# Ten orders of a step for the first 23 steps of a fused attention and two-MoE kernel, output banks freed of each other's copies, the tenth mask on TensorE, and the embeddings' norms moved to the first two steps

## The chip, the cores and the metric

The kernel runs on one core of a Trainium2 chip as one program. The time is that of the device in microseconds (us), the median of three runs. The engines are named as the profile names them: PE (TensorE's matmuls), PEld (its weight loads), DVE (VectorE), ACT (ScalarE), POOL (GpSimd) and SP (SyncE, which issues most DMAs).

## The reference

Three stages follow each other, all in float32.

```python
# 1: attention, 4 batches x 8 heads, 576 positions, 64 wide, only the 32 largest scores of a row
scores = matmul(q, k.transpose(0, 1, 3, 2)) / sqrt(64)
kth    = partition(scores, -32)[..., -32:-31]          # the 32nd largest of each row
attn   = softmax(where(scores >= kth, scores, -1e9))
x      = matmul(attn, v)  ->  2304 tokens x 512
# 2: first MoE: a dense layer 512 -> 2048 -> 512
h = x @ w_in
x = (h * clip(h + 3, 0, 6) / 6) @ w_out
# 3: second MoE: 8 experts, each token goes to one
logits = normalised(x) @ normalised(expert_emb).T / tau
e      = argmax(logits);  gate = softmax(logits)[e]
out    = gate * (relu(x @ w1[e]) @ w2[e])
```

## The kernel before

**Stages.** Attention and the first MoE run together in a loop of 76 steps; behind it comes the tail with the routing's last part and the experts. There are 72 units of attention, one a step: a unit is 256 rows (two tiles of 128) of a batch and head against its 576 keys. Step i works on several units at once:

- unit i: the scores by TensorE into PSUM (`scores`, L456 to L469), a copy of half of the columns to SBUF by ACT (`take`, L476 on ACT), and DVE's `pairs` (L485 to L489), which orders columns by two and so prepares the search of the 32nd largest;
- unit i-1: the search itself on DVE (`select`, L504 MAX8 and L507), and `bounds` on POOL (L512, L514), which makes the threshold;
- unit i-2: `relu` on ACT (L518, the op `bend`), `mask` on POOL (L533), or, for units below `VEILED` = 9, `veil` on TensorE instead (L526, L527), which adds the same term with matmuls into a PSUM bank;
- unit i-3: the exponentials on ACT (L541), the sums' inverse, and `scale` (none for units below 8, on ACT at L557 for units 8 to 15, on POOL at L559 from 16 on);
- unit i-4: transposes on TensorE (`turned`, L570), their copies by ACT (`keep`, L575), the product with the values (`values`, L591/L596) and the normalising into the first MoE's input (`finish`, L603 to L649).

**The first MoE.** Its products are made of three float32 matmuls each (high by high, high by low, low by high part). Groups of 256 tokens go through it, one after the other, each in eight parts q; from step 12 a step does one q: `s1` (L681, the hidden units), `gate` (ACT, L689), `swish` (DVE, L693), `large` (ACT, L697), `small` (POOL, L700), and a step later `s2` (L716), the output. `s2` keeps two output banks, `bank_y[:, 0]` and `bank_y[:, 1]`, one for each 128 of the 256 tokens, and adds 6 matmuls to each a q, 48 in all. At q = 7 the bank is finished and ACT copies it: `out_y(o)` is called right behind the last matmuls of bank o, with the copy at L734 (for the last group L728). There are nine groups.

**The weights.** In steps 0 to 32 the weights of the first MoE are loaded and split into high and low parts by DVE (`w_one`, L262 or L264; `w_two`, L274), ACT (`w_round`, L282, and `w_hi`, L296) and POOL (`w_add`, L288; `w_low`, L300), and the low parts go back to memory (L304), from which they are fetched as they are needed (L321).

**The order.** Each engine does its instructions in the order in which the program lists them. The scheduler changes none: the loop stands under a manual schedule, and `step` calls the ops one after another as a string of words says. The words are the ops above with their part's number (`take1` is the second half's copy, `s20` and `s21` are `s2` on bank 0 and 1, `load0` a weight's DMA, `load_k` that of a key, `lows` the casts of a key and query at L438 to L445 and L382/L383). There are strings for step 0, 1 to 2, 3 to 11, 12 to 15, 16 to 20, and then one for odd and one for even steps.

```python
names = (ZERO if i == 0 else FEW if i < 3 else FIRST if i < MOES else MID if i < 16
         else NEXT if i < WORDS else ODD if i % 2 else THEN).split()
for name in names:
    ops[name]()
```

**Waits between tiles.** A semaphore wait is put in where an instruction uses a tile that another engine wrote or read. `bank_y` is one tile with both banks.

**The embeddings.** The eight expert embeddings are normalised early: `embed` in five parts behind steps 4, 18, 19, 20 and 21 (their DMAs, the squares on ACT, a product with ones on TensorE, a square root at L200 on ACT, three small operations of DVE). The square root needs another table of functions on ACT than the exponentials.

Of the kernel before, what the change touches and what calls it, by code (L numbers as in the profile page):

```python
# [40 lines left out]
SIGNED = (4, 6, 8, 10, 12, 14, 16, 18)  # L41
VEILED = 9
PLAIN = 1
# [3 lines left out]
BEGUN = (0, 1, 2, 3, 5, 7, 9, 11, 13, 15, 17, 19, 21, 22, 24, 25, 27, 28, 30, 31, 32)  # L47
ZERO = ("turn0 s10 values s11 round0 lows xh5 pick0 load_k one1 mask0 gate xh s20 one0 aside xl swish need_v pick1 ship prep "
       "expo0 hi1 two0 score0 bend0 expo1 large round1 s21 turn1 small take0 keep0 veil1 score1 load0 turn2 load_q guard low1 "
       "pairs load1 add0 inverse xl5 xe5 two1 hi0 scale low0 keep1 mask1 bounds store0 veil0 store1 pick2 bend1 pick3 keep2 "  # L50
       "take1 xe add1 ")
FEW = ("pick0 one1 one0 lows bend1 s10 bend0 values turn0 veil1 s11 s20 round0 keep0 two0 load_k add0 turn1 xh aside mask0 "
       "score0 pick1 xh5 keep1 expo0 xl5 hi1 pick2 ship xl expo1 s21 load0 take0 low1 gate hi0 guard need_v mask1 keep2 inverse "
       "xe5 round1 two1 turn2 swish low0 add1 prep large load1 load_q veil0 score1 store0 xe pick3 scale store1 bounds take1 "
       "small pairs ")
FIRST = ("s10 turn0 expo0 load_k s11 xh5 veil1 one1 s20 round0 turn1 keep0 round1 score0 lows one0 expo1 two0 load0 turn2 guard "
       "gate swish two1 take0 pick0 pick1 aside keep1 pick2 keep2 score1 add0 ship bend0 values xl5 hi0 xh veil0 add1 inverse "
       "take1 pick3 low0 bend1 need_v xe5 xl hi1 load1 s21 mask0 scale pairs xe store0 low1 mask1 large small store1 bounds prep "
       "load_q ")
MID = ("expo0 pick0 turn0 turn1 s10 score0 load_k one0 round0 two0 one1 pick1 two1 keep0 add0 keep1 turn2 expo1 s11 take0 s20 "  # L60
       "load0 hi0 round1 lows guard score1 ship keep2 values low0 pick2 pick3 need_v inverse bend0 load1 add1 gate bend1 scale "
       "mask0 swish large bounds store0 mask1 s21 prep aside xh hi1 pairs low1 xl load_q xe small store1 take1 ")
NEXT = ("one0 expo0 round0 turn0 lows turn1 two0 s10 one1 s11 keep0 keep1 turn2 expo1 round1 bend0 score0 keep2 two1 load0 pick0 "
       "gate add0 guard hi0 values add1 pick1 take0 pick2 mask0 s20 inverse ship hi1 swish low0 low1 score1 load1 xh bend1 large "
       "scale pick3 load_k xl small mask1 bounds prep store0 s21 take1 aside store1 need_v pairs load_q xe ")
THEN = ("lows pick0 turn0 expo0 keep0 ship expo1 pick1 bend0 s10 guard turn1 place pick2 inverse score0 mask0 turn2 s11 take0 "
# [3 lines left out]
       "take0 swish values expo1 load_k score1 guard need_v pick3 bounds take1 large aside inverse s20 s21 scale small xh pairs "  # L70
       "prep xl load_q")
HS = S // 2
QS = S // 4
# [45 lines left out]
def layers(tc: tile.TileContext, qt, kt, v, w_in, w_out, embt, tau, w1, w2, out, y_dram, yq_dram, g_dram, tbl, xq_dram, lo_dram, flag, pools, consts):  # L119
# [59 lines left out]
    emb = {}  # L179

    def embed(part):

        if part == 0:
            emb["et"] = fs.tile([128, 4, E], F32, tag="df", name="et")
            nc.sync.dma_start(out=emb["et"], in_=embt.rearrange("(p k) e -> p k e", k=4))
            emb["tb"] = fs.tile([128, 1], F32, tag="gt", name="tb")
            nc.sync.dma_start(out=emb["tb"], in_=tau.rearrange("(o t) -> o t", o=1).broadcast_to([128, 1]))
        elif part == 1:
            emb["ones"] = mp.tile([128, DM], F32, tag="wf", name="onesf", bufs=4)[:, :128]
            nc.gpsimd.memset(emb["ones"], 1.0)  # L190
            emb["sq"] = fs.tile([128, 4, E], F32, tag="tmp", name="sq")
            nc.scalar.activation(emb["sq"], emb["et"], AF.Square)
        elif part == 2:
            onesf, sq = emb["ones"], emb["sq"]
            emb["pe"] = pe = half_a()
            for k in range(4):
                nc.tensor.matmul(pe[:, :E], onesf, sq[:, k, :], start=(k == 0), stop=(k == 3))
        elif part == 3:
            emb["nr"] = fs.tile([128, E], F32, tag="nrm", name="nr")
            nc.scalar.activation(emb["nr"], emb["pe"][:, :E], AF.Sqrt)  # L200
        else:
            nr = emb["nr"]
            nc.vector.tensor_scalar(nr, nr, 1e-6, emb["tb"][:, 0:1], op0=ALU.add, op1=ALU.mult)
            nc.vector.reciprocal(nr, nr)
            nc.vector.tensor_tensor(ent, emb["et"], nr.unsqueeze(1).broadcast_to([128, 4, E]), op=ALU.mult)
# [456 lines left out]
    def push_group(X, gs):  # L662
# [39 lines left out]
        def s2(q, part=None):  # L702
# [6 lines left out]
            for o in range(len(gs)):  # L709
# [3 lines left out]
                for a in range(2):  # L713
                    f = 2 * q + a
                    for n, (x, w) in enumerate(((gh, wh[:, f, :]), (gh, wl[:, a, :]), (gl, wh[:, f, :]))):
                        nc.tensor.matmul(state["y"][o], x[:, a, c], w, start=(f == 0 and n == 0), stop=(f == 15 and n == 2))  # L716
                if q == 7:
# [6 lines left out]
        def out_y(o):  # L724
            final = gs[o] >= NG - 2
            if final:
                t = late["xg"].tile([128, DM], F32, tag="xg", name="ysl")
                nc.scalar.copy(t, state["y"][o])  # L728
                nc.sync.dma_start(out=y_dram[128 * gs[o]:128 * gs[o] + 128, :], in_=t)
                finals.append((t, gs[o]))  # L730
                return
            if o == 0:
                state["t"] = stg.tile([128, 2, DM], F32, tag="st", name="ysb")
            nc.scalar.copy(state["t"][:, o, :], state["y"][o])  # L734
            if o == 1:
# [217 lines left out]
    def step(i, last):  # L953
# [23 lines left out]
        def after(o):  # L977
            if last:
# [5 lines left out]
                   guard=lambda: at_(3, guard), inverse=lambda: at_(3, inverse), scale=lambda: at_(3, scale), bounds=lambda: at_(1, bounds),  # L984
                   pairs=lambda: at_(0, pairs), values=lambda: both(values, False), xh5=lambda: fifth(finish), xl5=lambda: fifth(finish_low), xe5=lambda: fifth(finish_early), xh=lambda: both(finish), xl=lambda: both(finish_low), xe=lambda: both(finish_early))
        for n in range(2):
            ops["veil" + str(n)] = lambda n=n: at_(2 + n, veil, n)
# [8 lines left out]
        for name, f, j in (("load", w_load, -1), ("one", w_one, 0), ("two", w_two, 0), ("round", w_round, 0), ("add", w_add, 0),  # L996
                           ("hi", w_hi, 0), ("low", w_low, 0), ("store", w_store, 0)):
            for c in range(2):
                ops[name + str(c)] = lambda f=f, j=j, c=c: pair(f, j, c)
        names = (ZERO if i == 0 else FEW if i < 3 else FIRST if i < MOES else MID if i < 16 else NEXT if i < WORDS else ODD if i % 2 else THEN).split()  # L1000
        for name in names:
            ops[name]()
        if i in (4, 18, 19, 20, 21):
            embed((4, 18, 19, 20, 21).index(i))
        if i == 0:
# [9 lines left out]
    if True:  # L1015
        last = None
        with tc.manual_schedule():
            load_k(0)
            load_q(0, nc.scalar)
            w_load(0)  # L1020
            load_k(1)
# [3 lines left out]
            nc.gpsimd.tensor_scalar(tri, ident, -1.0, None, op0=ALU.mult)  # L1025
            nc.vector.memset(half, 0.5)
            nc.gpsimd.memset(kb[:, :, 0], -SCALE)
            nc.gpsimd.memset(kb[:, :, 1], BIG)
# [471 lines left out]
```

## Time and profile before

| what | value |
| --- | --- |
| median of three runs | 1011.04 us (1010.49 to 1011.4) |
| the profiled execution's own time | 1010.06 us |
| its span, first to last instruction | 1008.3 us |
| mean granted TensorE clock | 0.990 |
| busy: PE, PEld | 947.1 us (94%), 824.4 us (82%) |
| busy: DVE, ACT, POOL | 771.6 us (77%), 709.8 us (70%), 624.5 us (62%) |

The profiled execution stands 0.98 us below the median, and 1.8 us of it lie outside the span. A step is placed by the start of `pairs` in the trace: that of unit 0 starts at 6.68 us, of unit 15 at 142.13, of unit 19 at 190.35, of unit 22 at 219.56. The loop ends at about 725 us. The span in 40 slices of 25 us shows PE under 90% busy in the first seven and in the last one, and at 90% or more in all others; the shares by stage stand in the rows below.

### The profile page before, as it was taken

Reading aid. Unit: us, or ns where it says so; the run is one execution under the profiler, and the core shown is the slowest. Engines: PE = TensorE matmul, PEld = TensorE weight load, DVE = VectorE, ACT = ScalarE, POOL = GpSimd, SP = SyncE. Lnnn points to the kernel's source line nnn. Section 1 sums busy time; section 2 is a strip of 40 time slices with the busy share of each in tenths; the row PEclk is TensorE's granted clock in tenths of the full one; section 3 lists DMA queues with packets and bytes.
Section 4 is the critical chain, followed back from the end, with each engine's and each line's share of the span. In section 5 each row is a group of like instructions: output and inputs, shape, how many; then the busy total and the mean of one; then the engine's idle time right before and its main releaser. Section 6 shows DMA issues by size and latency. Waiting matters only on the chain. (4 is left out here: it accounts for less than half of the span.)

```text
span 1008.3 us, 20945 instructions
## 1 busy us (share of the span) xinstructions
PE 947.1 (94%) x7270; PEld 824.4 (82%) x7270; DVE 771.6 (77%) x2348; ACT 709.8 (70%) x1443; POOL 624.5 (62%) x793
## 2 busy tenths in 40 slices
PE   4787788999999999999999999999999999999997
PEld 2454577889889989988988888788898988999997
DVE  7999997889989989989989889882134455666661
ACT  5899898888789778789778777775334454555551
POOL 4799888867778788678688666666232453134310
PEclk9999799999999999999999999999999999999999
DMA  7666567653456654456565466466497567667730
GB/s 252 215 190 196 188 209 247 232 185 130 160 164 190 231 183 142 151 162 212 204 182 142 138 225 202 139 225 203 154 267 245 133 225 255 227 202 238 245 153 23
DMA packets 100691, 193.24 MB, mean 192 GB/s; under 512 B 16189, under 2 KB 42448, under 8 KB 100575
## 3 DMA queue, kind: packets, MB, share of 16 engines
q1 hardware_dynamic: 95983, 181.74, 55.8%
q0 software_dynamic: 4448, 10.00, 3.2%
q8 instruction: 59, 0.97, 0.4%
q14 instruction: 57, 0.47, 0.2%
q10 hardware_dynamic: 144, 0.07, 0.0%
HBM read 163.64 MB, written 24.92 MB: 187 GB/s over the span
## 5 line engine op out<-in xcount | busy, mean ns | idle before, releaser
L533 POOL TENSOR_TENSOR s<-s,z 128x576 f32<-128x576 f32 x126 | 162.5, 1290 | 62.5 <-ACT z L518 61.7
L681 PE MATMUL bank_h<-xh,vh 128*128 128x256 f32 x576 | 172.1, 299 | 0.0
L681 PE MATMUL bank_h<-xh,lo 128*128 128x256 f32 x576 | 164.3, 285 | 0.0
L681 PE MATMUL bank_h<-xl,vh 128*128 128x256 f32 x576 | 164.0, 285 | 0.0
L504 DVE MAX8 A<-left 128x8 f32<-128x288 f32 (+1 forms) x288 | 159.9, 598 | 0.0
L716 PE MATMUL bank_y<-wh,gh 128*128 128x512 f32 x288 | 117.6, 408 | 6.7 <-ACT ysb L734 6.0
L575 ACT COPY pt<-bank_t 128x384 f32<-128x384 f32 x216 | 101.6, 480 | 25.7 <-PE bank_t L570 25.6
L700 POOL TENSOR_TENSOR gl<-u,gh 128x512 fp32r<-128x512 f32 x72 | 93.3, 1296 | 42.0 <-ACT gh L697 41.8
L518 ACT ACTIVATE z<-s,nb 128x576 bf16<-128x576 f32 x144 | 112.9, 785 | 5.0 <-POOL nb L512 4.7
L570 PE MATMUL bank_t<-both,s 128*128 128x128 f32 x648 | 103.6, 277 | 13.0 <-ACT s L557 10.2
L716 PE MATMUL bank_y<-lo,gh 128*128 128x512 f32 x288 | 113.8, 395 | 0.0
L716 PE MATMUL bank_y<-wh,gl 128*128 128x512 f32 x288 | 113.4, 394 | 0.0
L681 PEld LDWEIGHTS bank_h<-xh,vh 128*128 128x128 f32 x576 | 111.4, 193 | 0.5 <-issue 0.2
L681 PEld LDWEIGHTS bank_h<-xl,vh 128*128 128x128 f32 x576 | 111.5, 194 | 0.3
L476 ACT COPY s<-ps_sc 128x576 f32<-128x576 f32 x143 | 92.3, 646 | 27.3 <-PE ps_sc L469 11.3
L681 PEld LDWEIGHTS bank_h<-xh,lo 128*128 128x128 f32 x576 | 111.0, 193 | 0.2 <-DMA lo<-lo_dram 0.2
L570 PEld LDWEIGHTS bank_t<-both,s 128*128 128x128 f32 x648 | 77.6, 141 | 35.7 <-ACT s L557 13.6
L541 ACT ACTIVATE s<-s,nb 128x576 f32<-128x576 f32 x126 | 99.1, 787 | 0.9 <-POOL s L533 0.9
L1118 POOL DMA_INDIRECT out_dram<-ob,idt x20 | 23.7, 1186 | 121.4 <-ACT ob L1111 81.6
L559 POOL TENSOR_SCALAR s<-s,sums 128x576 f32<-128x576 f32 x112 | 82.3, 746 | 18.1 <-DVE sums L548 17.6
L689 ACT ACTIVATE u<-bank_h,half 128x512 f32<-128x512 f32 x72 | 49.9, 693 | 61.8 <-PE bank_h L681 57.0
L941 DVE TENSOR_TENSOR l<-a,h 128x1024 fp32r<-128x1024 f32 x64 | 77.3, 1241 | 17.2 <-ACT h L939 17.2
(287 smaller groups left out, 2687.2 us busy)
## 6 DMA issues: line engine op xcount, KB each, us to landing
lo<-lo_dram SPq DMA_DIRECT2D x144, 512.0 KB, 4.8
a<-in_moe_w_dram SPq DMA_DIRECT2D x64, 512.0 KB, 6.7
vt<-in_v_dram SPq DMA_DIRECT2D x28, 320.0 KB, 5.3
w<-in_moe_w_in_dram SPq DMA_DIRECT2D x16, 512.0 KB, 4.6
lo_dram<-wf SPq DMA_DIRECT2D x32, 256.0 KB, 2.2
w<-in_moe_w_out_dram SPq DMA_DIRECT2D x16, 512.0 KB, 4.8
qraw<-in_q_dram SPq DMA_DIRECT2D x48, 128.0 KB, 4.1
krs<-in_k_dram SPq DMA_DIRECT2D x16, 288.0 KB, 4.1
```

Of the source, the lines that this page charges most:

```text
L476: nc.scalar.copy(sbuf[i % NS][:, :, HS * g:HS * g + HS], ps_[i][:, :, :HS])
L504: nc.vector.max(A[:, n, 8 * r:8 * r + 8], src[:, n, :w])
L518: nc.scalar.activation(zb_[n], tile_of(i, n), AF.Relu, bias=sel[i][1][:, n, 1:2], scale=-BIG)
L533: nc.gpsimd.tensor_tensor(s, s, zb_[n], op=ALU.subtract)
L541: nc.scalar.activation(s, x, AF.Exp, bias=sel[i][1][:, n, 0:1], scale=SCALE, accum_out=sums[i][:, n:n + 1])
L559: nc.gpsimd.tensor_scalar(x, x, rv[:, n:n + 1], 1.0, op0=ALU.mult, op1=ALU.mult)
L570: nc.tensor.transpose(pp[:, 128 * k:128 * k + 128], e[:, 128 * (3 * c + k):128 * (3 * c + k) + 128], ident)
L575: nc.scalar.copy(pts[i][:, 3 * c:3 * c + 3, :].rearrange("p k n -> p (k n)"), tb_.pop((i, c))[:, :384])
L681: nc.tensor.matmul(ph[:, a, :], w, x[:, k, :], start=(k == 0 and n == 0), stop=(k == 3 and n == 2))
L700: nc.gpsimd.tensor_tensor(state[q][1], state.pop((q, "u")).rearrange("p (a n) -> p a n", a=2), state[q][0].bitcast(F32), op=ALU.subtract)
L716: nc.tensor.matmul(state["y"][o], x[:, a, c], w, start=(f == 0 and n == 0), stop=(f == 15 and n == 2))
L941: nc.vector.tensor_tensor(lo, x, hi.bitcast(F32), op=ALU.subtract)
```

## The change

Four things change.

1. **Orders.** The five strings for steps 0 to 20 give way to ten, for steps 0; 1 to 2; 3 to 9; 10 to 11; 12 to 13; 14 to 15; 16 to 17; 18 to 20; 21; 22. From step 23 on the two strings are as before. The ops are the same; what each string changes is the order in which every engine finds them.
2. **Banks.** The matmuls of `s2` on one bank are declared independent of the copies that read the other bank.
3. **Tenth mask.** `VEILED` goes from 9 to 10: unit 9's mask, two instructions of POOL, becomes 8 matmuls of TensorE.
4. **Embeddings.** The DMAs of the embeddings are issued from ACT's queue ahead of the loop, the ones lie in a tile that is used otherwise only later, the squares are made ahead of the loop, and the product, the square root and a first use of the exponential (which brings its table back) are an op `root` in step 1. The last part stays behind step 21.

```diff
-VEILED = 9
+VEILED = 10
...
-ZERO = ("turn0 s10 values s11 round0 lows xh5 pick0 load_k one1 mask0 gate xh s20 one0 aside xl swish need_v pick1 ship prep "
...
+ORDERS = ((1, "turn0 lows one1 load0 pick0 ship keep0 score0 turn1 bend1 load_k hi1 xh5 s20 pick1 aside mask0 one0 values xh "
...
         if part == 0:
             emb["et"] = fs.tile([128, 4, E], F32, tag="df", name="et")
-            nc.sync.dma_start(out=emb["et"], in_=embt.rearrange("(p k) e -> p k e", k=4))
+            nc.scalar.dma_start(out=emb["et"], in_=embt.rearrange("(p k) e -> p k e", k=4))
...
         elif part == 1:
-            emb["ones"] = mp.tile([128, DM], F32, tag="wf", name="onesf", bufs=4)[:, :128]
+            emb["ones"] = norm_[:, 0, :128]
...
             nc.scalar.activation(emb["nr"], emb["pe"][:, :E], AF.Sqrt)
+            nc.scalar.activation(emb["sq"][:, 0, 0:1], half, AF.Exp)
...
-                        nc.tensor.matmul(state["y"][o], x[:, a, c], w, start=(f == 0 and n == 0), stop=(f == 15 and n == 2))
+                        w_ = nc.tensor.matmul(state["y"][o], x[:, a, c], w, start=(f == 0 and n == 0), stop=(f == 15 and n == 2))
+                        tc.declare_no_dep(w_.ins, group=f"bank {1 - o} {exact}", reason="the other bank is read")
...
-                nc.scalar.copy(t, state["y"][o])
+                w_ = nc.scalar.copy(t, state["y"][o])
+                tc.add_to_no_dep_group(f"bank {o} {exact}", w_.ins)
...
-            nc.scalar.copy(state["t"][:, o, :], state["y"][o])
+            w_ = nc.scalar.copy(state["t"][:, o, :], state["y"][o])
+            tc.add_to_no_dep_group(f"bank {o} {exact}", w_.ins)
...
+        ops["root"] = lambda: (embed(2), embed(3)) if i == 1 else None
...
-        names = (ZERO if i == 0 else FEW if i < 3 else FIRST if i < MOES else MID if i < 16 else NEXT if i < WORDS else ODD if i % 2 else THEN).split()
+        names = next((o for n, o in ORDERS if i < n), ODD if i % 2 else THEN).split()
         for name in names:
             ops[name]()
-        if i in (4, 18, 19, 20, 21):
-            embed((4, 18, 19, 20, 21).index(i))
+        if i == 21:
+            embed(4)
...
             load_q(0, nc.scalar)
+            embed(0)
             w_load(0)
...
             nc.vector.memset(half, 0.5)
+            embed(1)
```

On TensorE, at the eighth part of the second group (`s2`, L716; three rows to each of the 16 hidden blocks, `gh` and `gl` are the parts of the activations), the program of before has this. The last three rows of bank 0, then bank 1's six, then the transposes:

```order
L716 MATMUL bank_y<-wh,gh 128x512
L716 MATMUL bank_y<-lo_3375,gh 128x512
L716 MATMUL bank_y<-wh,gl 128x512
L716 MATMUL bank_y<-wh,gh 128x512 [waits Activation_49]
L716 MATMUL bank_y<-lo_3375,gh 128x512
L716 MATMUL bank_y<-wh,gl 128x512
L716 MATMUL bank_y<-wh,gh 128x512
L716 MATMUL bank_y<-lo_3375,gh 128x512
L716 MATMUL bank_y<-wh,gl 128x512
L570 MATMUL bank_t_119<-both,s_143 128x128 [waits Pool_49]
```

The same place now (L716 is now L737, L570 is L591):

```order
L737 MATMUL bank_y<-wh,gh 128x512
L737 MATMUL bank_y<-lo_3381,gh 128x512
L737 MATMUL bank_y<-wh,gl 128x512
L737 MATMUL bank_y<-wh,gh 128x512
L737 MATMUL bank_y<-lo_3381,gh 128x512
L737 MATMUL bank_y<-wh,gl 128x512
L737 MATMUL bank_y<-wh,gh 128x512
L737 MATMUL bank_y<-lo_3381,gh 128x512
L737 MATMUL bank_y<-wh,gl 128x512
L591 MATMUL bank_t_119<-both,s_143 128x128 [waits Pool_49]
```

The rows stay where they are; the wait of bank 1's first matmul for ACT is gone.

On ACT, in step 16 of before: from the last copies of transposes, by both halves of unit 16's scores (L476), to the first row behind them (`z` is made by `relu`, `u` and `gh` belong to the first MoE, `s_142` at L557 is the scale of unit 13, `qh` and `kst` are casts of the next query and key):

```order
L575 COPY pt<-bank_t_119 128x384
L689 ACTIVATE u<-bank_h,half 128x512
L296 CAST wh<-wf 128x512
L476 COPY s_141<-ps_sc 128x2x288
L518 ACTIVATE z_148<-s_143,nb 128x576
L697 CAST gh<-u 128x512
L557 ACTIVATE s_142<-s_142,sums 128x576 x2
L438 CAST qh<-qraw 128x256
L382 CAST kst<-kraw 128x576
L383 CAST kst<-kraw 128x576
L476 COPY s_141<-ps_sc 128x2x288
L541 ACTIVATE s_143,sums<-s_143,nb 128x576
```

Step 16 now (L689 is L710, L296 is L317, L476 is L497, L518 is L539, L697 is L718, L557 is L578, L438 is L459, L382 is L403):

```order
L539 ACTIVATE z_148<-s_143,nb 128x576
L539 ACTIVATE z_147<-s_143,nb 128x576
L596 COPY pt<-bank_t_118 128x384
L497 COPY s_141<-ps_sc 128x2x288
L596 COPY pt<-bank_t_119 128x384
L317 CAST wh<-wf 128x512
L710 ACTIVATE u<-bank_h,half 128x512
L459 CAST qh<-qraw 128x256
L403 CAST kst<-kraw 128x576
L404 CAST kst<-kraw 128x576
L497 COPY s_141<-ps_sc 128x2x288
L718 CAST gh<-u 128x512
```

Between the two copies of scores stood `z`, `gh` and the two scales beside the casts; now `z` stands ahead of both and `gh` and the scales (the two rows behind the last one shown) behind both. In the same step `load_k`, the key's DMA on SP, moves from behind the two weight loads to ahead of them.

On POOL, steps 11 and 12 of before (`s` at L533 is the mask of unit 9, `norm` and `xl` are the first MoE's input, `wf` weights, `nb` the thresholds):

```order
L632 TENSOR_TENSOR norm<-norm 128x128
L533 TENSOR_TENSOR s_142<-s_142,z_147 128x576
L649 TENSOR_TENSOR xl<-norm,xh 128x128
L300 TENSOR_TENSOR wf<-wf,vh 128x512
L533 TENSOR_TENSOR s_142<-s_142,z_148 128x576
L512 TENSOR_TENSOR nb<-A,kb 128x4
L514 TENSOR_TENSOR spare<-A 128x4
L288 TENSOR_TENSOR wf<-wf,w_1108 128x512
```

The same place now (L632 is L653, L649 is L670, L300 is L321, L512 is L533, L288 is L309):

```order
L653 TENSOR_TENSOR norm<-norm 128x128
L670 TENSOR_TENSOR xl<-norm,xh 128x128 x2
L321 TENSOR_TENSOR wf<-wf,wh 128x512
L321 TENSOR_TENSOR wf<-wf,vh 128x512
L533 TENSOR_TENSOR nb<-A,kb 128x4
L535 TENSOR_TENSOR spare<-A 128x4
L309 TENSOR_TENSOR wf<-wf,w_1116 128x512
```

The two masks are gone from POOL's queue; unit 9's masking is done by TensorE in steps 11 and 12.

## Rows read from the trace of the kernel before

**Rows 1.** Windows: start:end length, busy PE PEld DVE ACT POOL, clock, DMA share, GB/s.
```profile
6.68:142.13 135.45, 99.21 (x678) 66.27 (x680) 133.75 (x438) 118.56 (x243) 112.09 (x131) 0.95 0.63 207
15.18:31.93 16.75, 9.72 (x37) 5.04 (x37) 16.61 (x56) 12.21 (x22) 11.05 (x13) 1.00 0.82 263
58.50:102.80 44.30, 32.91 (x256) 21.61 (x256) 43.96 (x148) 41.84 (x92) 41.33 (x52) 1.00 0.63 200
102.80:122.04 19.24, 14.23 (x70) 10.06 (x72) 19.10 (x61) 16.64 (x33) 15.92 (x19) 0.73 0.48 165
142.13:181.12 38.99, 33.13 (x240) 28.14 (x237) 30.46 (x94) 34.46 (x71) 33.54 (x36) 0.96 0.72 218
181.12:219.56 38.44, 36.70 (x293) 32.56 (x293) 34.35 (x117) 31.62 (x66) 26.93 (x40) 1.00 0.63 210
219.56:725.00 505.44, 499.99 (x4257) 444.08 (x4256) 426.86 (x1470) 389.17 (x842) 362.39 (x500) 1.00 0.56 177
```

**Rows 2.** Waits of PE from 219.56 to 725 (us in total, times, longest).
```profile
PE bank_y L716 <- ACT ysb L734: 5.3, 7, 1.3
```

**Rows 3.** Waits of PEld over the whole span, the last group's output.
```profile
PEld bank_y L716 <- ACT ysl L728: 1.1, 1, 1.1
```

**Rows 4.** Timeline of one such wait: start, duration, engine, [idle before <-releaser].
```profile
281.78 1.47 POOL L559 TENSOR_SCALAR s<-s,sums 128x576 f32<-128x576 f32 x2
...
282.34 0.40 PE L716 MATMUL bank_y<-lo,gh 128*128 128x512 f32 x1
...
282.57 0.39 PE L716 MATMUL bank_y<-wh,gl 128*128 128x512 f32 x1
...
283.00 0.58 ACT L734 COPY ysb<-bank_y 128x512 f32<-128x512 f32 x1 [0.23 <-PE bank_y L716]
...
283.64 0.50 PE L716 MATMUL bank_y<-wh,gh 128*128 128x512 f32 x1 [0.67 <-ACT ysb L734]
...
283.97 0.40 PE L716 MATMUL bank_y<-lo,gh 128*128 128x512 f32 x1
...
285.13 0.38 PE L570 MATMUL bank_t<-both,s 128*128 128x128 f32 x2
```

**Rows 5.** Waits of PE from 142 to 220.
```profile
PE bank_t L570 <- ACT s L557: 2.5, 2, 1.8
...
PE bank_y L716 <- ACT ysb L734: 0.7, 1, 0.7
```

**Rows 6.** Waits of DVE from 142 to 200.
```profile
DVE ps_sc L485 <- ACT s L476: 8.8, 4, 4.4
```

**Rows 7.** Timeline of ACT in step 16.
```profile
151.26 0.78 ACT L518 ACTIVATE z<-s,nb 128x576 bf16<-128x576 f32 x1
...
153.79 0.39 ACT L438 CAST qh<-qraw 128x256 fp32r<-128x256 f32 x1
155.21 0.67 ACT L382 CAST kst<-kraw 128x576 fp32r<-128x576 f32 x1 [1.02 <-DMA kraw<-in_k_dram]
...
156.36 0.63 ACT L476 COPY s<-ps_sc 128x576 f32<-128x576 f32 x1
```

**Rows 8.** Timeline beside unit 9's first mask.
```profile
105.96 1.28 POOL L533 TENSOR_TENSOR s<-s,z 128x576 f32<-128x576 f32 x1
...
106.02 1.51 DVE L264 TENSOR_SCALAR wf<-w 128x512 int32<-128x512 int32 x1
```

**Rows 9.** DVE's instructions of line 264: duration in ns, minimum, median, maximum.
```profile
L264 DVE TENSOR_SCALAR wf<-w x24: 415/420/1509, 5.4 to 183.4; 128x512 int32<-128x512 int32 x24
```

**Rows 10.** Timeline of PE in a step with `veil` (step 7).
```profile
68.40 0.75 PE L526 MATMUL bank_y<-s,both 128*128 128x288 f32 x2 [1.16 <-ACT s L541]
...
69.11 0.65 PE L526 MATMUL bank_y<-s,both 128*128 128x288 f32 x2
```

**Rows 11.** Timeline of ACT at the square root of the norms.
```profile
199.21 1.28 ACT L200 ACT_TABLE_LOAD   x1
200.50 0.18 ACT L200 ACTIVATE nr<-bank_a 128x8 f32<-128x8 f32 x1
```

More of the change, by code (lines that the diff above doesn't have):

```diff
@@ L47 @@
 BEGUN = (0, 1, 2, 3, 5, 7, 9, 11, 13, 15, 17, 19, 21, 22, 24, 25, 27, 28, 30, 31, 32)
-ZERO = ("turn0 s10 values s11 round0 lows xh5 pick0 load_k one1 mask0 gate xh s20 one0 aside xl swish need_v pick1 ship prep "
[L49 to L65, printed above, removed]
 THEN = ("lows pick0 turn0 expo0 keep0 ship expo1 pick1 bend0 s10 guard turn1 place pick2 inverse score0 mask0 turn2 s11 take0 "
@@ L71 @@
        "prep xl load_q")
+ORDERS = ((1, "turn0 lows one1 load0 pick0 ship keep0 score0 turn1 bend1 load_k hi1 xh5 s20 pick1 aside mask0 one0 values xh "
[6 rows of a table added]
+             "add1 root store1 small scale pairs "),
[3 rows of a table added]
+             "scale store1 load_q bounds small "),
[3 rows of a table added]
+             "store0 bounds pairs store1 scale "),
[7 rows of a table added]
+             "aside "),
[3 rows of a table added]
+             "small "),
[3 rows of a table added]
+             "need_v "),
+          (22, "aside turn0 lows turn1 keep0 s10 pick0 expo0 ship bend1 pick1 expo1 s11 turn2 mask1 gate swish keep1 bend0 guard "
+             "s20 keep2 mask0 large small score0 load_k prep inverse pick2 values pick3 take0 need_v xh score1 take1 xl pairs "
+             "s21 scale load_q bounds place "),
+          (23, "turn0 s10 turn1 score0 expo0 keep0 s11 bend0 lows expo1 turn2 guard pick0 pick1 mask0 take0 pick2 inverse aside "
+             "s20 score1 need_v gate keep1 take1 pick3 keep2 swish pairs bend1 scale large load_k values bounds s21 xh load_q "
+             "ship place mask1 prep small xl "))
 HS = S // 2
@@ L184, in embed @@
             emb["et"] = fs.tile([128, 4, E], F32, tag="df", name="et")
-            nc.sync.dma_start(out=emb["et"], in_=embt.rearrange("(p k) e -> p k e", k=4))
+            nc.scalar.dma_start(out=emb["et"], in_=embt.rearrange("(p k) e -> p k e", k=4))
             emb["tb"] = fs.tile([128, 1], F32, tag="gt", name="tb")
-            nc.sync.dma_start(out=emb["tb"], in_=tau.rearrange("(o t) -> o t", o=1).broadcast_to([128, 1]))
+            nc.scalar.dma_start(out=emb["tb"], in_=tau.rearrange("(o t) -> o t", o=1).broadcast_to([128, 1]))
         elif part == 1:
-            emb["ones"] = mp.tile([128, DM], F32, tag="wf", name="onesf", bufs=4)[:, :128]
+            emb["ones"] = norm_[:, 0, :128]
             nc.gpsimd.memset(emb["ones"], 1.0)
```

25 rows, old and new, of the table ORDERS are left out of this document.

## The prediction

> **What bounds the kernel now.** I read the windows first, cut at the stages: rows 1 show three different limits. From 6.68 to 142.13 us (steps 0 to 15) DVE is busy 133.75 of 135.45 us, so 1.70 us are free on it and PE, with 99.21, waits for others. From 142.13 to 219.56 (steps 16 to 22) nobody is full: PE is busy 33.13 of 38.99 us, then 36.70 of 38.44, so it idles 5.86 and 1.74 us, and over the first piece the granted clock is 0.96 [rows 1]. From 219.56 to 725 PE is busy 499.99 of 505.44 us and sets the time [rows 1]. The page's own busy share of PE (94%) hides these three; what an edit is worth depends on the stage it falls in.
>
> Second I read who PE waits for in the PE-bound stage. There is one releaser only: ACT's copy of the output bank, 7 times, 5.3 us together [rows 2]. That is nearly all of the 5.45 us of idle time there. Third, the timeline of one such wait [rows 4], and then the waits and ACT's timeline in steps 16 to 22 [rows 5 to 7], and the collisions of DVE and POOL [rows 8, 9].
>
> **The banks (part 2).** In rows 4 the last matmul of bank 0 starts at 282.57; the copy of bank 0 runs from 283.00 for 0.58; the first matmul of bank 1 starts at 283.64. From start to start that is 1.07 us, where the neighbours, 282.34 to 282.57, take 0.23: 0.84 lost. The matmul behind the pause also takes 0.33 to its successor (283.64 to 283.97) where 0.23 is usual, another 0.10. So this wait costs 0.94, of which the row counts 0.67 as a wait: 0.27 more than a row of waits shows. The two banks share no data, and the order shows the wait gone and no other put in its place on these rows. Is something else late then? The next instruction of PE behind bank 1 is the transpose at 285.13, which waits for POOL's scale; that ends at 281.78 + 1.47 = 283.25, 1.88 us ahead, so a start 0.94 earlier still finds it done [rows 4]. ACT's copy runs while PE fills bank 1; what it delays on ACT is what it delays now, since its own start is set by bank 0's end. There are seven such waits behind 219.56 and one before it (0.7 us, rows 5), and one of the last group, which the weight loads show with 1.1 us [rows 3]. The seven give 5.3 by the table and 5.3 + 7 x 0.27 = 7.2 with what it leaves out. The other two give 0.94 each, so 9.1 in all. One of them lies in steps where PE isn't full, so I take **8.6**, with bounds of 5.0 (the table's 5.3 less something that comes late) and 9.1.
>
> **The orders in steps 16 to 22 (part 1).** The upper bound is all idle time of PE there: 5.86 + 1.74 = 7.6, less the 0.7 of the bank = 6.9; and if PE never paused the clock would hold at 1.00 instead of 0.96, 0.04 x 38.99 = 1.6 more: 8.5 [rows 1, 5]. What of it the new order takes can be followed in one place. DVE waits 8.8 us in four pieces for ACT's copy of scores, up to 4.4 at once [rows 6]; that one is step 16. There the copy of the second half stands at 156.36 behind z, gh and two scales, which fill ACT from 151.26 to 153.79 = 2.53 us, and behind the casts of the next key, which wait 1.02 for that key's DMA [rows 7]. The order of now has z ahead of both copies, gh and the scales behind both, and the key's DMA is issued ahead of the two weight loads on SP instead of behind them. So 2.53 + 1.02 = 3.55 us leave the way of this copy. The price: the scale is now last on ACT in its step, while the transposes which need it come early in the next step on PE, and PE already waits for that scale twice, 2.5 us in total [rows 5]. In steps 18 to 22 I can follow no single change of this size. I take **3.5** for these seven steps, the row followed best, with bounds of -3 (the wait for the scale doubled, 2.5, and a little of the first piece given back) and 8.5.
>
> **The orders in steps 0 to 15 (part 1).** The same instructions stay on DVE, so its 133.75 us can shrink only where one is stretched now. Line 264 shows this: its 24 instructions take 0.42 in the median and up to 1.51 [rows 9], and the longest, at 106.02, runs beside POOL's mask from 105.96 to 107.24 [rows 8]: 1.09 more than it needs. Above, I bound the gain by two such stretches and all of DVE's 1.70 idle: 3.9. The mask of unit 9 leaves POOL for good, so the 1.09 go unless another two-input instruction of POOL takes that place. I take **1.1**, with bounds of -3 and 3.9. The lower end is three new collisions of 1.09, since the strings of these steps are new throughout.
>
> The Trainium skill, SBUF — State Buffer, section "Who interferes with whom", says that VectorE and GpSimd share ports under an exclusive lock and that the loser waits for the winner's whole instruction. Rows 8 agree: the DVE instruction that started 0.06 behind the mask ended 0.29 behind it. By that rule any of the new strings can win or lose as much, which the fourth rival works out from the rows.
>
> **The tenth mask (part 3).** TensorE gets four more pairs of rows like those at 68.40 and 69.11, 0.71 apart: 4 x 0.71 = 2.9 us [rows 10]. They fall in steps 11 and 12, where PE is busy 14.23 of 19.24 us [rows 1]: 5.0 idle cover it, also at the clock of 0.73 of that stretch (2.9 / 0.73 = 4.0). So **0**; without the cover it would cost 2.9. The two instructions of 1.28 leave POOL, busy 15.92 of 19.24 and not the bound; what that is worth on DVE is counted above.
>
> **The embeddings (part 4).** The square root with its table and the table back take 1.28 + 0.18 + 1.28 = 2.74 us of ACT [rows 11], the load back counted as long as this one. They leave steps 19 and 20, which is part of the idle time counted above, and come into steps 1 and 2, where ACT is busy 12.21 of 16.75 [rows 1]: 4.5 us of idle time hide them there, though in one piece, so ACT's copies of scores may come 2.7 late once. DVE is busy 16.61 of 16.75 there and would feel that. I take **-0.1** between 0 and -2.7.
>
> **The sum.** 8.6 + 3.5 + 1.1 + 0 - 0.1 = 13.1 us. The profiled execution takes 1010.06, which becomes 997.0; the median stands 0.98 above it (1011.04), so I forecast **998.0**.
>
> **The rivals.**
> First, another wait takes the bank's place: PE arrives up to 0.94 earlier at an instruction whose producer isn't earlier. For it: all of PE's slack in 505 us was this wait, so the others have never been tested. Against: rows 4 show 1.88 us of margin at the next wait. Half of the bank's gain is then lost: 998.0 + 4.3 = 1002.3. Chance 8%.
> Second, the orders bring nothing, gains and losses even out, and only the banks count: 1011.04 - 8.6 = 1002.4. For it: in steps 0 to 15 DVE has almost nothing to give, and in steps 16 to 22 I followed one place out of many. Against: 8.8 us of DVE's waiting have one cause, which is moved. Chance 18%.
> Third, ACT becomes the bound of the early steps. In steps 6 to 10 it is busy 41.84 of 44.30 us [rows 1]; a string that puts one more instruction of 0.63 [rows 7] ahead of the scores' copy than before makes DVE wait that long in each step. Over the 12 steps 3 to 14 that is 7.6: 998.0 + 7.6 = 1005.6. Chance 6%.
> Fourth, on the slower side: in steps 3 to 15 the new strings put one DVE instruction of a step beside a two-input instruction of POOL, where it waits as at 106.02, 1.09 each [rows 8]. Thirteen steps make 14.2, and 998.0 + 14.2 = 1012.2. The place is fixed by the string and so would come every step; that is for it. Against it: 23 of the 24 instructions of line 264 met less than that, though DVE and POOL are both busy over 80% of this stage [rows 1], so such meetings are rare. It decides the sign from 13.1 / 1.09 = 12 collisions on. Chance 6%.
>
> **How the numbers follow.** The forecast has 62%, with its own range of 993.5 to 1002.5. The whole range, 991 to 1005, adds the first two rivals and leaves out the third and fourth and the far ends of the unknown costs (bounds of 8.5 and 3.9 both reached would give 990). What differs by less than 0.2%, 2 us, a measurement of this kernel can't tell from no change. Slower by more than that needs the fourth rival or an unseen loss of 15: 5%. Within it lies the weaker half of that rival together with the lower bounds of both order terms: 4%. Faster: 91%.
>
> **What would show it.** In the profile after, the wait of bank_y for the copy has no row in PE's waits between the stages' ends, and the stretch from unit 22's `pairs` to the loop's end is 7 us shorter (banks). `pairs` of unit 22 starts about 5 us earlier than 219.56: some 1 by unit 15 and 4.5 by unit 22 with the one bank wait in it (orders). DVE's longest instruction of line 264 is under 1.51 and PE has idle time left from step 10 to 12 (mask). DVE has no new pause in steps 1 and 2 of over 0.5 us (embeddings). The forecast is wrong if the PE-bound stage shortens by less than 4 us, since then a new wait has come, or if unit 15's `pairs` starts later than 142.13, since then the early orders cost DVE time.

## The result and the profile after

The changed kernel takes 994.01 us in the median of six runs (992.9 to 995.0), where the kernel before took 1010.95 beside it (1010.49 to 1011.74): a ratio of 0.9832, 95% interval 0.9819 to 0.9845, or 17 us less. The forecast was 998.0 with 991 to 1005. The profiled execution takes 995.0 (span 993.3), the slowest of the six; against the profiled one of before it is 15.06 us shorter, where the sum said 13.1.

The starts of `pairs` (DVE, L485 before, L506 after) show where. This table is worked out from the two traces; the last rows are ACT's last copy of the first MoE's output (L728, now L750), the issue of the last scatter and the span.

| point | before | after | difference |
| --- | --- | --- | --- |
| unit 6 | 58.50 | 59.12 | +0.62 |
| unit 15 | 142.13 | 141.97 | -0.16 |
| unit 16 | 157.03 | 153.65 | -3.38 |
| unit 18 | 181.12 | 174.60 | -6.52 |
| unit 19 | 190.35 | 185.11 | -5.24 |
| unit 22 | 219.56 | 211.50 | -8.06 |
| unit 70 | 665.06 | 650.82 | -14.24 |
| last output copy | 770.21 | 753.96 | -16.25 |
| last scatter issued | 1002.99 | 986.69 | -16.30 |
| span | 1008.3 | 993.3 | -15.0 |

So nothing by unit 15, 7.9 us in steps 16 to 22, and 8.2 from there to the last output copy, most of it in eight steps of 0.97, one at each group's end. At the very end 1.2 us go back: the last scatter lands 4.6 us behind its issue instead of 3.4.

The windows after, cut at the same units as [rows 1] (length, busy time of PE, PEld, DVE, ACT, POOL, then the clock):

```profile
6.84:141.97 135.13, 106.82 (x691) 69.85 (x693) 132.46 (x437) 121.75 (x248) 109.83 (x129) 0.96 0.67 214
103.51:122.32 18.81, 15.11 (x107) 11.30 (x106) 18.45 (x60) 17.17 (x35) 13.93 (x17) 0.82 0.53 173
141.97:174.60 32.63, 29.12 (x242) 25.66 (x239) 30.46 (x96) 32.05 (x67) 29.95 (x33) 1.00 0.70 225
174.60:211.50 36.90, 35.95 (x292) 32.66 (x291) 34.79 (x119) 30.74 (x66) 30.82 (x42) 1.00 0.73 238
211.50:711.40 499.90, 499.35 (x4269) 445.77 (x4268) 426.77 (x1470) 390.66 (x845) 362.56 (x500) 1.00 0.57 180
```

In the PE-bound stage 5.45 us of idle have become 0.55. PE's waits there show what the 0.55 is, one late weight:

```profile
PE bank_y L737 <- DMA lo<-lo_dram: 0.6, 1, 0.6
```

The place of [rows 4], on PE, ACT and POOL: bank 1's first matmul now starts 0.23 behind bank 0's last, while ACT copies bank 0, and the transpose behind the bank (L591) follows at once, POOL's scale (L580) having ended at 275.14:

```profile
273.67 1.47 POOL L580 TENSOR_SCALAR s<-s,sums 128x576 f32<-128x576 f32 x2
...
274.45 0.39 PE L737 MATMUL bank_y<-wh,gl 128*128 128x512 f32 x1
...
274.68 0.39 PE L737 MATMUL bank_y<-wh,gh 128*128 128x512 f32 x1
...
274.88 0.59 ACT L757 COPY ysb<-bank_y 128x512 f32<-128x512 f32 x1 [0.21 <-PE bank_y L737]
...
276.05 0.49 PE L591 MATMUL bank_t<-both,s 128*128 128x128 f32 x3
```

DVE's waits from 142 to 192 us: of the 8.8 us for ACT's copies of scores in [rows 6], 0.6 are left:

```profile
DVE ps_sc L506 <- ACT s L497: 0.6, 1, 0.6
```

And ACT in step 16, the place of [rows 7]: no wait for the key's DMA any more, and the copy at 152.93 follows the casts at once, with gh and the scales behind it:

```profile
151.48 0.45 ACT L459 CAST qh<-qraw 128x256 fp32r<-128x256 f32 x1
151.78 0.73 ACT L403 CAST kst<-kraw 128x576 fp32r<-128x576 f32 x1
...
152.93 0.69 ACT L497 COPY s<-ps_sc 128x576 f32<-128x576 f32 x1
153.46 0.68 ACT L718 CAST gh<-u 128x512 fp32r<-128x512 f32 x1
153.97 1.50 ACT L578 ACTIVATE s<-s,sums 128x576 f32<-128x576 f32 x2
```

The price that was feared, PE waiting for that scale, is 1.5 us in two waits from 141.97 to 211.50, where [rows 5] have 2.5 in two:

```profile
PE bank_t L591 <- ACT s L578: 1.5, 2, 1.1
```

### The profile page after: what moved, and what is told of

Read it like the earlier page. It is cut to its first block, busy times and chain, and to the rows that moved or that the text cites. A ratio compares the mean times of both kernels' runs of the same rounds, so it can differ in the third digit from the quotient of the medians.

```text
span 993.3 us, 20958 instructions
## 1 busy us (share of the span) xinstructions
PE 947.3 (95%) x7282; PEld 825.9 (83%) x7282; DVE 770.3 (78%) x2348; ACT 710.4 (72%) x1444; POOL 621.8 (63%) x791
## 5 line engine op out<-in xcount | busy, mean ns | idle before, releaser
L554 POOL TENSOR_TENSOR s<-s,z 128x576 f32<-128x576 f32 x124 | 159.6, 1288 | 58.8 <-ACT z L539 57.9
L737 PE MATMUL bank_y<-wh,gh 128*128 128x512 f32 x288 | 115.8, 402 | 0.0
L539 ACT ACTIVATE z<-s,nb 128x576 bf16<-128x576 f32 x144 | 111.4, 779 | 4.8 <-POOL nb L533 4.2
L737 PE MATMUL bank_y<-lo,gh 128*128 128x512 f32 x288 | 113.0, 392 | 0.6 <-DMA lo<-lo_dram 0.6
L737 PE MATMUL bank_y<-wh,gl 128*128 128x512 f32 x288 | 112.8, 392 | 0.0
L497 ACT COPY s<-ps_sc 128x576 f32<-128x576 f32 x143 | 92.2, 645 | 28.1 <-PE ps_sc L490 12.4
L591 PE MATMUL bank_t<-both,s 128*128 128x128 f32 x648 | 102.0, 278 | 5.5 <-ACT s L578 4.4
L591 PEld LDWEIGHTS bank_t<-both,s 128*128 128x128 f32 x648 | 77.5, 142 | 24.5 <-ACT s L578 6.4
L710 ACT ACTIVATE u<-bank_h,half 128x512 f32<-128x512 f32 x72 | 49.8, 692 | 62.3 <-PE bank_h L702 57.5
L580 POOL TENSOR_SCALAR s<-s,sums 128x576 f32<-128x576 f32 x112 | 82.4, 747 | 18.7 <-DVE sums L569 18.2
L617 PE MATMUL bank_a<-pt,vt 128*64 128x128 f32 (+1 forms) x1600 | 89.3, 267 | 2.5 <-ACT pt L596 2.5
```

What stands on the lines that cost most here:

```text
L497: nc.scalar.copy(sbuf[i % NS][:, :, HS * g:HS * g + HS], ps_[i][:, :, :HS])
L539: nc.scalar.activation(zb_[n], tile_of(i, n), AF.Relu, bias=sel[i][1][:, n, 1:2], scale=-BIG)
L554: nc.gpsimd.tensor_tensor(s, s, zb_[n], op=ALU.subtract)
L580: nc.gpsimd.tensor_scalar(x, x, rv[:, n:n + 1], 1.0, op0=ALU.mult, op1=ALU.mult)
L591: nc.tensor.transpose(pp[:, 128 * k:128 * k + 128], e[:, 128 * (3 * c + k):128 * (3 * c + k) + 128], ident)
L617: nc.tensor.matmul(av[64 * n:64 * n + 64, c0:c1], vt[:, k, 64 * n:64 * n + 64], pt[:, k + 5 * n if k < 4 else 4, c0:c1], start=(o == 0), s ...
```

## The experiments

Times are medians of device time with the ratio to the kernel before on the same chip and its interval. The two chips of the last eight runs are slower behind the loop (the kernel before takes 1015 us there). In the trace of the changed kernel taken on one of them, the stretch from unit 71 to the last scatter's issue is 332.6 us long, not 325.6, with PE idle for 6.2 of it instead of 1.6. Intervals are wide there, so those runs are read by the places of units. From unit 15 on these repeat: the gain from unit 15 to unit 22, against the first trace of before, is 7.90 and 7.91 in two traces of the changed kernel. I call it **G** below, and G16 and G18 the same at units 16 and 18 (3.22 and 6.36). All G lean on one trace of before, in which step 16 was slower than in a second trace with the same string (0.48, see the early strings); the difference between two G does not.

**The banks alone.**

```diff
+ (before) tc.declare_no_dep(...) and tc.add_to_no_dep_group(...) at L716, L728, L734 as in the change; nothing else
```

> The kernel before with the banks declared free of each other's copies and nothing else. Theory (the parts add up): the PE-bound stretch of the changed kernel is 6.9 us shorter, one wait more lies ahead of it and one in the last group, 0.96 each, so 8.8 us are gained: about 1002.2, and no row of PE waiting for ysb is left. The pairs of unit 22 come 0 to 1 us earlier than 219.56. Rival 1 (another wait takes its place in the old order): half of it, about 1006.5. Rival 2 (the gain needs the new orders): under 2 us, about 1010.

1000.58 us, ratio 0.9911 (0.9897 to 0.9925): 9.0 less. Unit 22 stands 0.96 earlier against unit 21, and from there on each group's end gives 0.97, as the theory has it. It is neither halved nor does it need the orders.

**The banks undone.**

```diff
- (after) the same two declarations
```

> The changed kernel with the banks' declaration taken out, all else as it is. Theory (the parts add up): 8.8 us longer than the changed kernel's 994.0, about 1002.8, with the eight waits for ysb and the one for ysl back at 0.9 to 1.0 each. Rival (with new orders PE has other slack that absorbs the waits): 997 to 999.

1000.57 us, ratio 0.9908 (0.9895 to 0.9922). From unit 22 to unit 70 the difference to before stays between 9.7 and 10.1, no steps of 0.97 any more, and PE's and PEld's waits over the whole span have them back:

```profile
PE bank_y L737 <- ACT ysb L755: 5.4, 7, 1.3
PEld bank_y L737 <- ACT ysl L749: 1.1, 1, 1.1
```

Seven waits, not eight: G is 7.91 here too, so the first group's bank costs nothing with the new orders. It is worth 0.96 with the old ones only. That fits 9.0 alone and 0.9908 - 0.9832, or 7.7, in company, though the intervals are too wide to prove it.

**Late strings alone, early strings alone.** In the first the second half of unit 9's mask (4 of 8 matmuls) is left out, since the old string has no word for it in step 12; the exponentials there read other numbers.

```diff
- names = next((o for n, o in ORDERS if i < n), ...)
+ (late_orders)  ZERO, FEW with root, FIRST, MID for i < 16, else as in the change
+ (early_orders) ORDERS for i < 16, NEXT, ODD and THEN behind it
```

> The changed kernel with the old strings for steps 0 to 15 and the new ones for steps 16 to 22 (banks, tenth mask and the early norms stay; the norms' op stands in step 1 of the old string). Theory (the early strings are worth nothing by themselves, the 7 us come in steps 16 to 22): 993 to 995, pairs of unit 15 at 141.5 to 142.5, of unit 22 at 211 to 212. Rival (the late strings live on what the early ones leave ready, such as weights split earlier): half of the 7 us lost, 997 to 998, with unit 15 where it was and unit 22 at 215.

> The changed kernel with the new strings for steps 0 to 15 alone; steps 16 to 22 have the old ones (banks, tenth mask and early norms stay). Theory (the gain is made in steps 16 to 22 by their strings): 7.1 us longer than the changed kernel's 994.0 less what the norms' leaving gives, so 999 to 1001, pairs of unit 22 at 216.5 to 218.6. Rival (the early strings and the norms' leaving make most of it): 994 to 997, pairs of unit 22 at 212 to 215.

Late: 994.04, ratio 0.9849 (0.9835 to 0.9863); unit 15 at 142.15, G 7.89. The late strings need nothing of the early ones, and the ratio is 1.7 us behind the changed kernel's, within the intervals. Early: 995.80, ratio 0.9870 (0.9854 to 0.9885), G 4.01. So the strings of steps 16 to 22 are worth 7.90 - 4.01 = 3.9. The other 4.0 come without them: 0.8 and 1.2 at units 20 and 21, 0.96 at unit 22 (the bank) and 1.07 at unit 16, where 0.48 also came with the banks alone. These two are the key's wait of [rows 7]. Step 16 has the old string in all three traces, and ACT waits for the key 1.02 in the first trace of before, 0.55 with the banks alone and not at all here. The casts of query and key in ACT's timeline, with the banks alone and then here:

```profile
153.58 0.40 ACT L438 CAST qh<-qraw 128x256 fp32r<-128x256 f32 x1
154.53 0.68 ACT L382 CAST kst<-kraw 128x576 fp32r<-128x576 f32 x1 [0.55 <-DMA kraw<-in_k_dram]
```

```profile
151.65 0.39 ACT L477 CAST qh<-qraw 128x256 fp32r<-128x256 f32 x1
151.95 0.67 ACT L421 CAST kst<-kraw 128x576 fp32r<-128x576 f32 x1
```

So this wait is worth its length at unit 16. About half of it comes and goes with the execution, for with the banks alone nothing ahead of it was changed; here the key is issued 5.81 us behind unit 15 instead of 6.26. By the forecast numbers the rival is met (995.8, unit 22 at 213.35), with unit 15 2.2 early in that trace. By G it is half and half: the late strings make 3.9 of 7.9, and the ratios of this kernel and the changed one are about as far apart (0.9870 - 0.9832, 3.8 us).

**The changed kernel again.** It tells what varies from one execution to the next from what is the kernel's own.

> The changed kernel again, on the chip of the three runs beside it. In the first trace of it the pairs of unit 6 come 0.6 us late against before, in two kernels with the same strings for steps 0 to 15 they come 0.95 early; the end of the last scatter lies 6.6 us behind its issue, elsewhere 5.3 to 5.6. Theory (both are scatter from one execution to the next, on the DMAs' side): here unit 15 stands at 139.9 to 142.2 and the median is 16 to 17 us under that of before. Rival (both belong to this kernel): unit 15 at 142, the last scatter 6.6.

998.90, ratio 0.9828 (0.9801 to 0.9854), unit 15 at 140.46 and unit 6 at 57.57. The first theory holds for unit 15: in the eight traces whose steps 0 to 15 are those of the changed kernel it stands 0.16, 1.81, 2.20, 1.67, 0.24, 1.04, 0.73 and 1.96 earlier than in the first trace of before, 1.2 in the mean; with the old strings and nothing else changed there, at 0, 0.21 earlier and 1.64 later. In the first trace after, a copy of scores came 0.4 late for DVE in step 3 and a weight 0.5 late in step 5; in this one neither did. The slow last scatter did not come back: from its issue to the end of the span it is 5.7 us here, 6.6 in the first trace and 5.3 to 6.6 across the kernels.

**The embeddings late.**

```diff
- (after) embed(0), embed(1) ahead of the loop, root in step 1
+ embed's parts behind steps 4, 18, 19, 20, 21 as before
```

> The changed kernel with the embeddings' five parts as before: DMAs on SP behind step 4, the rest behind steps 18 to 21. Theory (the norms' leaving is worth 2.0 us, as the old strings show it where it gains 0.8 and 1.2 at units 20 and 21): 1.5 to 2.5 us longer than the changed kernel, all of it between units 19 and 22. Rival (as the prediction had it, the new strings hide them: worth nothing beyond idle time): within 0.5.

1000.95, ratio 0.9853 (0.983 to 0.9877). G is 5.98, so 1.92 are lost, and all behind unit 19 (5.11 there against 5.09 in the changed kernel). The rival falls.

**Only the square root late.**

```diff
-            nc.scalar.activation(emb["nr"], emb["pe"][:, :E], AF.Sqrt)
-            nc.scalar.activation(emb["sq"][:, 0, 0:1], half, AF.Exp)
+            nc.scalar.activation(emb["nr"], emb["pe"][:, :E], AF.Copy)
...
+        if i == 20:
+            nc.scalar.activation(emb["nr"], emb["nr"], AF.Sqrt)
```

> The changed kernel with the product of the norms early in step 1 as it is, copied out there, and only the square root, with its two table loads, behind step 20 as before. Theory (ACT's 2.7 us for tables and root make the 1.9 us that the late norms cost): 1.5 to 2.0 us later at unit 22 against unit 15 than in the changed kernel. Rival (the product's 2.04 us of TensorE cost it, in a stage where TensorE is nearly full): under 0.5.

998.96, ratio 0.9835 (0.9815 to 0.9855). G is 6.41: 1.5 of the 1.9 are ACT's, through ACT's two loads (ACT's timeline)

```profile
191.94 1.28 ACT L1028 ACT_TABLE_LOAD   x1
193.24 0.21 ACT L1028 ACTIVATE nr<-nr 128x8 f32<-128x8 f32 x1
193.35 0.46 ACT L595 COPY pt<-bank_t 128x384 f32<-128x384 f32 x1
193.83 1.28 ACT L561 ACT_TABLE_LOAD   x1
```

behind which the gate's activation came late for DVE (DVE's waits from 138 to 225; 0.9 without the late root):

```profile
DVE u L713 <- ACT u L709: 2.6, 1, 2.6
```

The other 0.4 go with the product and the two parts that were late as well; they were not parted.

**Unit 9's mask on POOL.** In the string for steps 10 and 11 the words of the two masks change places, so that each stands behind the relu it needs.

```diff
-VEILED = 10
+VEILED = 9
```

> The changed kernel with unit 9's mask back on POOL, its two instructions each behind the relu that they need in the string of steps 10 and 11. Theory (the mask on POOL stretches DVE's instruction beside it, worth 0.8 at unit 12): 0.7 to 1.1 us longer up to unit 15, and less than that at the end if PE then binds. Rival (the new string keeps DVE's weights' step away from the masks): within 0.3 at unit 15.

999.53, ratio 0.9843 (0.9818 to 0.9868). Against the changed kernel's second trace unit 11 comes 1.69 later and unit 15 2.58; G is 7.98, so none of it is given back by unit 22. The theory had the right sign, and only the smaller part of the mechanism. The stretch is there: the instruction of line 285 that takes 0.42 in the changed kernel (at 105.25) starts beside the unit's second mask and ends 0.29 behind it, 0.53 longer (POOL's timeline, then DVE's):

```profile
106.32 1.28 POOL L554 TENSOR_TENSOR s<-s,z 128x576 f32<-128x576 f32 x1
```

```profile
106.94 0.95 DVE L285 TENSOR_SCALAR wf<-w 128x512 int32<-128x512 int32 x1
```

The larger part stands ahead of it, the 1.69 at unit 11, where ACT's copy of scores comes late (here DVE in step 11):

```profile
103.70 0.47 DVE L506 TENSOR_TENSOR ps_sc<-ps_sc,s 128x288 f32<-128x288 f32 x1 [1.78 <-ACT s L497]
```

In POOL's queue stands the first mask, itself behind a wait of 0.90 for ACT's relu, and behind it all that follows, down to the `norm`; for that ACT waits ahead of that copy (POOL's timeline, then ACT's):

```profile
97.98 1.29 POOL L554 TENSOR_TENSOR s<-s,z 128x576 f32<-128x576 f32 x1 [0.90 <-ACT z L539]
...
102.15 0.45 POOL L653 TENSOR_TENSOR norm<-norm 128x128 f32<-128x128 f32 x1
```

```profile
102.63 0.50 ACT L669 CAST xh<-norm 128x128 fp32r<-128x128 f32 x2 [1.46 <-POOL norm L653]
103.04 0.63 ACT L497 COPY s<-ps_sc 128x576 f32<-128x576 f32 x1
```

**One step of the old string.** Step 16 of before alone.

```diff
+ (before, i == 16) ... two1 load_k load0 ... prep store0 s21 take1 large small scale aside ...
- ... two1 load0 ... bend1 large scale pick3 load_k xl small ... s21 take1 aside ...
```

> The kernel before with another string in step 16 alone: the key's DMA ahead of the weights' DMAs, and gh, gl and the scales (large, small, scale) behind the second copy of scores. Theory (what filled ACT ahead of that copy cost 3.5 us, of which z's 0.8 stays): pairs of unit 16 come 2.0 to 2.8 us earlier, and unit 18 keeps at least 1.5 of it. Rival 1 (the late scale holds the transposes of the next step and gives it back): under 0.5 left at unit 18. Rival 2 (the copy waits for TensorE's scores or for the DMA anyway): unit 16 within 0.5 of 157.0.

1014.81, ratio 0.9998 (0.9982 to 1.0014): no difference that can be told on that chip. By places, unit 16 comes 2.97 earlier against unit 15, and unit 18 keeps 1.69. Unit 15 stood 1.64 late in this trace, and unit 18 is where it was before (0.05 earlier). Part of the 1.69 may thus be a late start made up for, why step 17 gives 1.27 back isn't shown, and the step alone settles nothing beyond unit 16. There the 2.97 fit the key's wait and what the next run finds for gh and the scales, 1.07 and 1.83.

**The scales first.** Steps 16 and 17 of the changed kernel.

```diff
- (after) load1 take1 swish hi1 s21 aside large guard bounds xl load_q mask0 inverse low1 xe scale pairs
+ load1 swish large guard inverse scale take1 hi1 s21 aside bounds xl load_q mask0 low1 xe pairs
```

> The changed kernel with gh and the two scales ahead of the second copy of scores in steps 16 and 17, as before. Theory (what fills ACT ahead of that copy makes DVE wait): gh and two scales are 0.6 + 1.4 = 2.0 us, so unit 16 stands 1.5 to 2.0 later against unit 15 than in the changed kernel and unit 18 keeps at least 1.5. Rival (PE's transposes get the scale earlier for it, which pays it back): under 0.5 left at unit 18.

1000.11, ratio 0.9853 (0.9831 to 0.9876). `swish`, `guard` and `inverse`, which gh and the scales need, move with them. G16 is 1.39 instead of 3.22: 1.83 later, as the theory has it, and 2.64 at unit 18. It isn't paid back. DVE waits for the copy 4.6 us from 138 to 225, against 1.1:

```profile
DVE ps_sc L505 <- ACT s L496: 4.6, 4, 2.4
```

**The key late.**

```diff
- (after) turn2 load_k s11 ... gate prep add1 ... s20 store0 load1 take1
+ turn2 s11 ... gate add1 ... s20 store0 load1 load_k prep take1
```

> The changed kernel with the key's DMA behind both weights' DMAs on SP in steps 16 and 17, as before, and its cast behind it. Theory (the wait of 1.02 for the key stood in the way of the second copy of scores): pairs of unit 16 come 0.7 to 1.5 us later against unit 15 than in the changed kernel, those of unit 17 more. Rival (ACT has other work to wait with, or the DMAs land in time anyway): under 0.3.

1008.62, ratio 0.9933 (0.9915 to 0.995): far beyond both. Unit 16 comes 6.7 us later than in the changed kernel (against unit 15), unit 22 13.2. The edit also put the key's DMA behind `store0`. On SP that store waits for POOL's low part, and the key behind it:

```profile
145.73 0.40 SPq L270 DMA_DIRECT2D w<-in_moe_w_in_dram  x1
151.47 0.32 SPq L324 DMA_DIRECT2D lo_dram<-wf  x1
151.89 0.38 SPq L270 DMA_DIRECT2D w<-in_moe_w_in_dram  x1
152.32 0.49 SPq L395 DMA_DIRECT2D kraw<-in_k_dram  x1
```

ACT then stands for it, ahead of the copy of scores:

```profile
157.65 0.67 ACT L402 CAST kst<-kraw 128x576 fp32r<-128x576 f32 x1 [6.83 <-DMA kraw<-in_k_dram]
```

In the changed kernel the key is issued at 146.30, before the weights. So the run shows what the key's place on SP can cost, but not the 1.02 by itself, which the traces beside the early strings show.

**Steps 16 and 17 alone.**

```diff
+ (after) NEXT for steps 18 to 20, ODD and THEN from 21
```

> The changed kernel with the old strings for steps 18 to 22, so that of the late strings only that for steps 16 and 17 is new. Theory (steps 16 and 17 make the gain, and from unit 19 on TensorE is full, so that the later strings neither add nor lose much): from unit 15 to unit 22 it gains 7.4 to 8.4 us against before, as the changed kernel does with 7.9. Rival 1 (the gains of the old strings with the norms gone, 2.0 between units 17 and 21, come on top of the 6 made by unit 17): 9 us or more, and a kernel faster than the changed one by 0.7 or more. Rival 2 (each new string gives its share): under 6.5.

999.2, ratio 0.983 (0.9809 to 0.9852). G is 6.44. The theory's 7.4 is missed, and the second rival's bound of 6.5 is just met: unit 18 has 3.48 instead of 6.36, and the old strings get 3.0 back behind it. The ratio can't tell these 1.5 us from nothing; in the traces they still stand at unit 70. The first rival, which would have been the better kernel, falls; nothing here beats the changed one.

## Why the prediction was right, point by point

The direction, the three places and the size within 4 us were right; the terms were not all the right size. By the places of units and the runs:

| term | forecast | measured | from |
| --- | --- | --- | --- |
| banks | 8.6 | 9.0 alone; 7.7 in company | the two bank runs |
| strings of steps 16 to 22 | 3.5 with the key's wait | 3.9 without it | G with and without them |
| the key's wait in step 16 | 1.02 of the 3.5 | 1.07, about half with the execution | unit 16 with the early strings alone |
| embeddings' norms | -0.1 | 1.9 | the late embeddings |
| strings of steps 0 to 15 with the mask | 1.1 | 0.2 to 2.2, mean 1.2 | eight traces |

With the mean in the last row the measured terms add up to 15.8 to 17.1, beside 16.9 of the medians.

**Banks.** A wait costs 0.97, not 0.94, and no other took its place (first rival): from unit 22 to unit 70, with six of the waits between them, the time is 6.2 shorter. The margin of 1.88 at the transposes was enough: they start 0.24 behind the last matmul. The bank in the first group is the one that was said to lie "in steps where PE isn't full", and it is hidden once the strings are new.

**Steps 16 to 22.** The step that was followed holds: 3.55 was predicted for unit 16 and 3.2 came. Of these, 1.83 are gh and the scales, and 1.07 are the key's wait, which also went without the new string; z, which now stands ahead of both copies, is left with 0.3. What the prediction couldn't follow, steps 17 to 22, gave 2.4 more at unit 17, took 1.3 back at unit 19 (PE idles 0.7 of 10.5 us there) and gave 2.6 at unit 22; the strings from step 18 on are 1.5 of G. The clock came as the upper bound had it: 1.00 in the first piece instead of 0.96.

**The embeddings, the step that failed.** "They leave steps 19 and 20, which is part of the idle time counted above": it was in the upper bound of 8.5 and was left out of the value taken. ACT has idle time there, but among the new strings the loads stand ahead of the gate's activation, and PE, busy 35.95 of 36.90 and then 499.35 of 499.90 us in the changed kernel, can't make up the 1.9. The product of the norms on PE was not priced at all. Among the old strings the gate is only 0.4 late for DVE at a time; of the 2.0 that leave with the norms between units 18 and 21 there, 1.0 is PE's work (26.41 against 25.44 us) and 1.0 its idle time. In steps 1 and 2 they cost nothing: one piece of 3.0 us on ACT, behind which the copy of scores comes at 18.99,

```profile
15.74 1.28 ACT L220 ACT_TABLE_LOAD   x1
...
18.52 0.20 ACT L221 ACTIVATE sq<-half 128x1 f32<-128x1 f32 x1
18.99 0.64 ACT L497 COPY s<-ps_sc 128x576 f32<-128x576 f32 x1 [0.27 <-PE ps_sc L486]
```

and DVE, in the middle of its search, meets no wait there: unit 2 starts at 23.35, before at 23.36.

**The mask.** It was read through the stretch of one DVE instruction, beside the second of the unit's two masks ([rows 8] call it the first). That stretch went: the instruction at that place takes 0.42, and line 285's longest, elsewhere, is 1.12. Unit 12 gained 0.8 against unit 11. With the late strings alone, where the steps around it have their old strings, it gained 1.12, the 1.09 that were forecast, and 0.6 of them are left by unit 15. But in the new string the same mask would cost 2.6 by unit 15, and only 0.53 of stretch is in them; more comes by POOL's queue, 1.69 by unit 11. The Trainium skill, SBUF — State Buffer, section "Who interferes with whom", names the lock as the price of such neighbours. The 0.53 agree with it, but the order of the queue was the larger price here. TensorE's matmuls (4 x 0.71 is 2.84; the prediction has 2.9) cost nothing, as forecast: PE is busy 15.11 of 18.81 us there.

**The rivals.** The second (only the banks) falls by G, the third and fourth by unit 15, which came no later in any of the eight traces. The 17 us in the medians against 15.06 in the traces lie in which executions were profiled: that of before stands 0.9 under its median, this one 1.0 above its own. In its trace the last scatter is 1.2 longer, a weight is 0.5 late in step 5 and another 0.55 at 650; what the other executions have of this isn't known.

## What to carry to other kernels

A wait that stands alone in a full stage is worth its whole start-to-start gap times its count, and the margin at the next wait says whether it stays gone. A cost that "lies in idle time" of an engine is free only if nothing of the bound engine's work stands behind it in that engine's queue; ask what is next in the queue, not how busy the engine is. The same holds for the queue that issues DMAs: a load behind a store that waits is as late as the store.

## What the hardware showed beside it

The early steps scatter from one execution to the next by more than the early strings are worth: unit 15 starts 2.0 us apart in eight traces of the same strings. DVE's waits up to there add up to 1.5 us in the two latest of them, 0.5 of it in one a weight, and to 0.2 in the two earliest. But from unit 15 to unit 22 the two traces of the changed kernel agree within 0.01. The last scatter, one DMA, landed 3.4 us after its issue in one execution and 4.6 in another. And the tail differs by chip: PE's waits there, in the changed kernel on one of the two slower ones, have a row that is 2.8 to 5.3 in all eight traces from these two, and 0.4 in both first traces:

```profile
PE ph L1071 <- DVE hl L1077: 5.0, 3, 2.6
```
